# Moving one group's output stores behind the transposes of the next groups, and two matmuls one place forward, in a fused attention and MLP kernel

## Chip, cores and metric

One NeuronCore of a Trainium2 chip. The metric is the device time of one execution in microseconds (us), of the slowest core, which here is the only one.

## The reference, cut to what matters

```python
kv  = einsum('bhsd,bhse->bhde', k, v)          # 8 batches, 8 heads, 576 rows, 64 wide
out = einsum('bhsd,bhde->bhse', q, kv)
x   = out / sqrt(mean(out*out) + 1e-6) * g_norm  # -> 4608 tokens x 512
h   = x @ w_in                                  # 512 -> 2048
g   = where(h > 0, h, exp(min(h, 0)) - 1)       # ELU
y   = g @ w_out                                 # 2048 -> 512, float32 out
```

## The kernel before

The 4608 tokens are worked in nine groups T of 512. For each group: x is made (attention, scaling, and for T >= 2 four DMA transposes of x with a multiplication by the gain after them), the first product gives h, ACT and DVE make the ELU, the second product gives y, ACT copies y from PSUM, SyncE issues the stores. Batch b of Q, K, V is fetched ahead by loads from GpSimd's queue; Q is turned by DMA transposes. All DMA transposes and nearly all stores are issued from SyncE, in program order.

```python
outp = ctx.enter_context(tc.tile_pool(name="outp", bufs=3))   # y tiles, 128 x 2 x 512 f32

def scale():                       # inside attention(T), for each half h of the group
    # DVE: xs = at * ss
    for i in (2 * h, 2 * h + 1):
        nc.sync.dma_start_transpose(out=xT[T][:, :, i*P : i*P+P], in_=st["xs"][:, i, :])
def gain():                        # DVE: xT[T][half h] *= g_col
    ...
def mm2_out(T, j):
    half = j // 2
    if j % 2 == 0:
        o_sb[T, half] = outp.tile([P, 2, DM], FP32, name="o_sb", tag="o")
    nc.scalar.copy(o_sb[T, half][:, j % 2, :], o_ps[T, j])
    if j % 2 == 1:
        store(T, half)             # two DMAs of 256 KB on SyncE
# ---- group 0, first product (tiles (i, a) of h, chunk c of the 4 of the contraction) ----
    early([(2, 1)], 0)
    early([(2, 1)], 2)
    early([(0, 0), (0, 1)], 3)     # the last chunk of the first pair; then ACT may start its ELU
    early([(2, 1)], 1)
    early([(1, 0), (1, 1), (2, 0), (2, 1)], 3)
# ---- ... group 1's first product, with attention(2) in between ----
    at["mul1"]()                   # group 2's second half of x: DVE scale, two transposes
    # cut: rest of group 1's ELU
    turn_q(3)                      # two DMA transposes of batch 3's Q
    after_turn(3)                  # GpSimd waits here for them
    fetch_ahead(4)                 # loads of batch 4: Q 1152 KB, K and V 576 KB each
    # cut: second product of group 1
    at["gain0"](); at["gain1"]()
# ---- group T = 2, eight pairs i of the first product, attention(3) in between ----
    early = {2: ("sum0", "inv0"), 5: ("sum1", "inv1", "mul1"), 6: ("gain0",), 7: ("gain1",)}
    late = {0: ("kv",), 1: ("se0",), 2: ("mul0",), 4: ("se1",), 5: ("ahead",)}
    # "early" runs ahead of the pair's ELU on DVE, "late" behind it
```

## Time and profile before

| | |
|---|---|
| timed executions before the prediction | 285.20, 285.07, 284.92 us |
| the profiled execution | **286.17 us**, span of the core 284.4 us |
| PE busy | 276.9 us, 97% of the span |

The span runs from the first to the last instruction; the device time was 1.8 us above it. The page, the chain of waits, the timeline and the DMA view are quoted in the prediction below.

### The profile page before, as it was taken

What the parts mean: (1) busy time and instruction counts of PE and PEld (TensorE: products, weight loads), DVE (VectorE), ACT (ScalarE), POOL (GpSimd) and SP (SyncE); (2) the same over time, 40 slices, a digit from 0 to 9 for tenths busy, and PEclk for the clock granted to TensorE, in tenths of its full rate; (3) what the DMA queues carried; (4) which work ended last, traced back from release to release, by engine and by line L of the source; (5) the groups of instructions that cost most, each with busy time, mean ns of one, the idle gap of its engine ahead of it and who ended that gap; (6) DMA issues with size and microseconds to landing.
All of it is one profiled execution on the core that took longest, in us unless ns stands there. A gap on an engine that the chain in (4) does not pass through costs nothing.

```text
span 284.4 us, 5154 instructions
## 1 busy us (share of the span) xinstructions
PE 276.9 (97%) x2123; PEld 129.1 (45%) x2123; DVE 164.4 (58%) x222; ACT 141.4 (50%) x209; POOL 47.9 (17%) x89
## 2 busy tenths in 40 slices
PE   8899999999899999999999999999999999999994
PEld 3444444444544444444444444444444444444443
DVE  2549532966487657754785378627863786344600
ACT  3778359594468255435542555345543554333311
POOL 7743303303330033033003120000000000000000
PEclk9999999999999999999999999999999999999999
DMA  7999999999896889779627971612150234020222
GB/s 208 198 203 207 206 263 236 174 298 144 191 282 72 163 182 239 94 176 262 148 37 172 248 173 35 157 37 74 37 113 0 74 39 111 0 76 0 74 74 75
DMA packets 50571, 39.46 MB, mean 139 GB/s; under 512 B 30964, under 2 KB 44020, under 8 KB 50548
## 3 DMA queue, kind: packets, MB, share of 16 engines
q0 software_dynamic: 15008, 21.30, 37.4%
q1 hardware_dynamic: 35136, 17.31, 29.4%
q10 hardware_dynamic: 404, 0.53, 0.5%
q8 instruction: 16, 0.26, 0.3%
q14 instruction: 7, 0.06, 0.1%
HBM read 36.70 MB, written 9.44 MB: 162 GB/s over the span
## 4 chain that ended last, share of the span: by engine, by line
PE 87%; DMA 6%; DVE 2%; ACT 2%; POOL 1%; issue 0%; SPq 0%; DVEq 0%; POOLq 0%
PE h_ps L382 40%; PE o_ps L403 40%; DMA xT<-xs 3%; DMA v_bf<-in_v_dram 3%; PE at L250 2%; PE at L156 1%; PE o_ps L440 1%; PE h_ps L569 1%; ACT elu_e L350 1%; DVE gT L366 1%; POOL k_bf L90 1%; PE mean L199 0%; PE qt_ps L174 0%; PE kv_ps L156 0%; PE y_ps L189 0%; DVE ss L283 0%
## 5 line engine op out<-in xcount | busy, mean ns | idle before, releaser
L403 PE MATMUL o_ps<-w_out_sb,gT 128*128 128x512 bf16 x560 | 129.7, 379 | 0.0
L382 PE MATMUL h_ps<-xT,w_in_sb 128*128 128x512 bf16 (+1 forms) x560 | 128.0, 376 | 1.0 <-DVE xT L312 0.9
L350 ACT ACTIVATE elu_e<-h_ps 128x1024 bf16<-128x1024 f32 (+1 forms) x79 | 74.0, 952 | 90.6 <-PE h_ps L382 89.0
L403 PEld LDWEIGHTS <-gT 128*128 128x128 bf16 x560 | 54.4, 98 | 65.8 <-issue 0.9
L382 PEld LDWEIGHTS <-w_in_sb 128*128 128x128 bf16 x560 | 53.2, 98 | 62.4 <-PE o_ps L403 1.4
L366 DVE TENSOR_TENSOR gT<-elu_e,h_ps 128x1024 bf16<-128x1024 bf16 (+1 forms) x67 | 77.2, 1157 | 6.9 <-PE h_ps L382 0.5
L362 DVE TENSOR_SCALAR elu_e<-elu_e 128x1024 bf16<-128x1024 bf16 x72 | 31.2, 433 | 64.6 <-ACT elu_e L350 64.6
L419 ACT COPY o_sb<-o_ps 128x512 f32<-128x512 f32 x32 | 18.3, 587 | 21.1 <-PE o_ps L403 21.1
L103 POOL CAST q_bf<-st_q 128x384 bf16<-128x384 f32 x36 | 16.8, 508 | 41.6 <-DMA st_q<-in_q_dram 41.6
L283 DVE TENSOR_REDUCE ss<-sq 128x16 f32<-128x1024 bf16 x14 | 17.1, 1220 | 6.8 <-ACT sq L277 6.8
L299 DVE TENSOR_TENSOR xs<-at,ss 128x1024 bf16<-128x1024 f32 x14 | 17.1, 1219 | 1.9 <-ACT ss L292 1.9
L277 ACT ACTIVATE sq<-at 128x1024 bf16<-128x1024 f32 x14 | 14.4, 1029 | 0.0
L212 DVE SCALAR_TENSOR_TENSOR xT<-y_ps,g_col,rT 128x512 bf16<-128x512 f32 (+1 forms) x10 | 6.2, 641 | 10.1 <-ACT rT L209 7.9
L339 POOL COPY gate<-qT 1x16 bf16<-1x16 bf16 x5 | 1.1, 217 | 59.0 <-DMA qT<-q_bf 59.0
L355 ACT ACTIVATE elu_h<-h_ps 128x1024 bf16<-128x1024 f32 (+1 forms) x12 | 9.3, 817 | 0.0
L156 PEld LDWEIGHTS <-k_bf 64*64 64x64 bf16 x576 | 6.4, 107 | 5.5 <-issue 5.5
L312 DVE TENSOR_SCALAR xT<-xT,g_col 128x1024 bf16<-128x1024 bf16 x14 | 6.7, 480 | 3.3 <-DMA xT<-xs 3.3
L90 POOL DMA_DIRECT2D v_bf<-in_v_dram x11 | 7.7, 700 | 4.2 <-DMA w_in_sb<-in_moe_w_in_dram 2.1
L90 POOL DMA_DIRECT2D k_bf<-in_k_dram x11 | 7.7, 704 | 2.6 <-DMA w_in_sb<-in_moe_w_in_dram 1.8
L250 PEld LDWEIGHTS <-qT 64*128 64x128 bf16 (+1 forms) x248 | 4.3, 97 | 6.1 <-issue 5.9
L112 DVE COPY o_sb<-o_ps 128x256 f32<-128x256 f32 x1 | 0.4, 424 | 11.1 <-PE o_ps L440 11.1
L366 DVE TENSOR_TENSOR gT<-elu_e,elu_h 128x1024 bf16<-128x1024 bf16 x9 | 6.2, 692 | 0.8
(57 smaller groups left out, 101.3 us busy)
## 6 DMA issues: line engine op xcount, KB each, us to landing
st_q<-in_q_dram POOLq DMA_DIRECT2D x6, 1152.0 KB, 8.4
out_dram<-o_sb SPq DMA_DIRECT2D x24, 256.0 KB, 3.4
k_bf<-in_k_dram POOLq DMA_DIRECT2D x6, 576.0 KB, 10.5
v_bf<-in_v_dram POOLq DMA_DIRECT2D x6, 576.0 KB, 12.6
out_dram<-o_sb SPq DMA_DIRECT2D x19, 128.0 KB, 2.4
w_out_sb<-in_moe_w_out_dram POOLq DMA_DIRECT2D x4, 512.0 KB, 15.4
w_in_sb<-in_moe_w_in_dram POOLq DMA_DIRECT2D x2, 512.0 KB, 10.7
q_bf<-in_q_dram POOLq DMA_DIRECT2D x3, 288.0 KB, 13.4
```

The source lines that it names most:

```text
L90: eng.dma_start(out=dst.rearrange("p m j d -> p m (j d)"), in_=in_[:, ms, :])
L103: nc.gpsimd.tensor_copy(out=bf["q", b][:, u, js], in_=raw[b][:, u::2, js, :].rearrange("p l j d -> p j l d"),)
L250: nc.tensor.matmul(se_ps[lo:hi, l, (4 * i + m) * 64 : (4 * i + m) * 64 + 64], lhsT=qT[b][l * 64 : l * 64 + 64, s, u, j : j + n, :], rhs=kv ...
L277: nc.scalar.activation(sq, st["se", h], AF.Square)
L283: nc.vector.reduce_sum(out=ss, in_=st.pop(("sq", h)).rearrange("p l (m e) -> p (l m) e", e=D), axis=AX.X,)
L299: nc.vector.tensor_tensor(out=st["xs"][:, 2 * h : 2 * h + 2, :].rearrange("p i (l m e) -> p l i m e", l=2, e=D), in0=se_ps.rearrange("p l ...
L350: nc.scalar.activation(e[:, lo:hi, :], h, AF.Exp)
L362: nc.vector.tensor_scalar(out=e, in0=e, scalar1=1.0, scalar2=1.0, op0=ALU.min, op1=ALU.subtract)
L366: nc.vector.tensor_tensor(out=gT[T][:, 2 * i + lo : 2 * i + hi, :], in0=e[:, lo:hi, :], in1=h, op=ALU.add if relu else ALU.max,)
L382: nc.tensor.matmul((ps[a] if isinstance(ps, list) else ps[:, a, :])[:, cols], lhsT=w_in_sb[:, c, f * P : f * P + P], rhs=xT[T][:, c, cols] ...
L403: nc.tensor.matmul(o_ps[T, j], lhsT=gT[T][:, f, j * P : j * P + P], rhs=w_out_sb[:, f, :], start=(f == 0), stop=(f == FC - 1),)
L419: nc.scalar.copy(o_sb[T, half][:, j % 2, :], o_ps[T, j])
```

## The change

The intent: group 0's stores (1 MB) stand ahead of group 2's transposes of x in SyncE's queue and share the DMA engines with batch 3's loads. They are issued later, behind those transposes and behind Q of batch 3, and a fourth output buffer keeps the tiles meanwhile. And the first pair of group 0's first product gets its last chunk one matmul sooner, so that its ELU starts sooner.

```diff
-    outp = ctx.enter_context(tc.tile_pool(name="outp", bufs=3))
+    outp = ctx.enter_context(tc.tile_pool(name="outp", bufs=4))
@@ mm2_out
-        if j % 2 == 1:
+        if j % 2 == 1 and T > 0:
             store(T, half)
@@ first product of group 0
     early([(2, 1)], 0)
+    early([(0, 0), (0, 1)], 3)
     early([(2, 1)], 2)
-    early([(0, 0), (0, 1)], 3)
     early([(2, 1)], 1)
@@ between group 1's first and second product
     turn_q(3)
+    for half in range(2):
+        store(0, half)
     after_turn(3)
```

## The prediction

> **What bounds the kernel now.** I read the page first: the tensor engine (PE) is busy 97% of a span of 284.4 us, at full granted clock in all 40 slices. So nearly everything that can still be won is time in which PE stands still, and there is little of it.
>
> ```profile
> span 284.4 us, 5154 instructions
> PE 276.9 (97%) x2123; PEld 129.1 (45%) x2123; DVE 164.4 (58%) x222; ACT 141.4 (50%) x209; POOL 47.9 (17%) x89
> PE 87%; DMA 6%; DVE 2%; ACT 2%; POOL 1%; issue 0%; SPq 0%; DVEq 0%; POOLq 0%
> ```
>
> The 7.5 us in which PE is not busy: PE's first matmul starts at 1.2 us and its last ends at 280.5 us, so about 5 us lie before and after the stream and are not touched. Some 2.5 us are left. In the chain that ended last only one DMA wait lies behind the first 20 us, 8.6 us long, and it is for a transpose of x. In order of time, from DVE's scaling to PE's next product:
>
> ```profile
> 60.12 1.22 DVE xs L299
> ...
> 62.62 8.60 DMA xT<-xs
> ...
> 71.32 0.50 DVE xT L312
> ...
> 71.91 1.92 PE h_ps L382 x16
> ```
>
> The timeline of the same place shows what PE loses by it (the last columns are the idle time before a row and what ended it), and that two DVE gains wait for the transposes, one for each half of x:
>
> ```profile
> 71.32 0.49 DVE L312 TENSOR_SCALAR xT<-xT,g_col 128x1024 bf16<-128x1024 bf16 x1 [2.16 <-DMA xT<-xs]
> 71.91 1.92 PE L382 MATMUL h_ps<-xT,w_in_sb 128*128 128x256 bf16 x16 [0.94 <-DVE xT L312]
> 72.26 0.49 DVE L312 TENSOR_SCALAR xT<-xT,g_col 128x1024 bf16<-128x1024 bf16 x1 [0.45 <-DMA xT<-xs]
> ```
>
> PE's idle time understates the loss. A stream of 8 matmuls of 512 columns takes 1.73 us in the chain, 0.216 us each, but one is booked 0.379 us, because ends are modelled. The last product before the wait started at 70.60, so the next was due at 70.81; it started at 71.91. The loss is **1.10 us**.
>
> The same test of starts elsewhere: after the start-up (18 us) only one other start is late by more than 0.2 us, the fifth pair of the first product (group 0), waiting for the PSUM pair that the first pair's ELU frees:
>
> ```profile
> 16.88 0.88 DVE L212 SCALAR_TENSOR_TENSOR xT<-y_ps,g_col,rT 128x256 bf16<-128x256 f32 x2 [0.45 <-ACT rT L562]
> 18.62 1.03 ACT elu_e L350
> 19.68 0.44 DVE elu_e L362
> 20.21 1.23 DVE gT L366
> 21.48 7.07 PE h_ps L382 x32
> ```
>
> The matmul before 21.48 started at 21.01, so this one was due at 21.23: **0.25 us** lost. The change's two parts aim at these two places.
>
> **Why the transposes are late.** In the DMA view of 48 to 71 us, sizes and the median time from issue to landing:
>
> ```profile
> st_q<-in_q_dram POOLq DMA_DIRECT2D x1, 1152.0 KB, 11.3
> out_dram<-o_sb SPq DMA_DIRECT2D x4, 256.0 KB, 4.1
> v_bf<-in_v_dram POOLq DMA_DIRECT2D x1, 576.0 KB, 16.6
> ```
>
> Group 0's four stores (1 MB) are issued at 51.05 to 54.6; batch 3's loads of Q, K, V (2.3 MB) at 52.66, 53.41 and 54.14. V lands at 54.14 + 16.6 = 70.7. The first two transposes of x, issued at 61.37 and 62.62, took 9.1 and 8.6 us and landed at 70.4 and 71.2: when the loads were through. The next two took 4.8 and 4.0 (71.7 and 72.2). Group 3's transposes at 91.5 and 92.7, with nothing else under way, took 2.4 to 2.5. The next batch's loads, issued at 74.25, had 0.5 MB of stores beside them, not 1 MB, and landed after 7.2 (Q) and 12.5 us (V).
>
> **What the Trainium skill says.** "DMA: Bandwidth & Descriptors", section "Issuing engines are not separate DMA queues": transfers issued from several engines run on the same 16 DMA engines and interleave. Its section "Queues, rings and completion order" has each DMA engine take turns between the queues with work, a packet at a time. The trace agrees about sharing: loads lengthen from 12.5 to 16.6 us beside twice the stores. It shows that a transpose does worse than a fair turn: 8.6 to 9.1 us beside loads, 2.4 alone. "TensorE: Matmul & The Clock Gate", section "Step-by-step: what each phase is for", gives 215.7 ns between starts of 512-column matmuls; the trace has 0.216 us.
>
> **The change, part by part.** No instruction is added or removed; PE has the same 2,123 matmuls. Comparing the order of instructions, SyncE's queue now has Q's transposes for batch 2, x's four, Q's two for batch 3, then the four stores; PE swaps one matmul with two.
>
> *Stores later.* Batch 3's loads keep their issue time, since their gate waits for Q's transposes of batch 2, which are ahead of the stores in both. Without stores they should do at least as well as the next batch's: Q at 52.7 + 7.2 = 59.9, V at 54.1 + 12.5 = 66.6 (an estimate from those rows). x's first two transposes then land by 67. DVE is in order, and its last ELU piece ahead of the first gain ends at 69.16, so that gain ends at 69.7: 1.1 us before PE wants it at 70.8. The third and fourth transposes wait for DVE's second scaling (66.90) and go out at 66.9 and 68.2 as before; at the undisturbed 2.5 us the fourth lands at 70.7 and the second gain ends at 71.2. PE needs it after 8 matmuls of 256 columns, 8 x 0.108 = 0.86 us behind 70.81, at 71.7. Half a microsecond to spare. So 1.10 us go; all of it lies on PE's path, and PE has no late start over 0.15 us behind 73 us, so it should reach the end whole.
>
> *Last chunk sooner.* The pair's last matmul moves up by one, so ACT's exponential, DVE's two steps and the released pair come 0.216 us sooner. But the first of the two now starts at 17.77, just when DVE ends that chunk (16.88 + 0.88 = 17.76); DVE's signal took 0.05 us at 16.43 to 16.48, so PE loses about 0.05 there. Net 0.25 - 0.05 = **0.20 us**.
>
> *The fourth output buffer* lets the deferred tiles stay; it is no work. It also removes a wait of ACT's copy for DVE, which had long been served.
>
> Sum: 1.10 + 0.20 = 1.30 us of 285.07, so 283.8 us.
>
> **The rivals.**
>
> 1. *The crowd moves to the next group.* The stores now go out at about 73 to 75, with group 1's store and batch 4's loads: 1.5 MB of stores beside 2.3 MB. V of that batch landed at 88.2; by 1 MB at the 246 to 249 GB/s that the DMA moved over 51 to 62 and 74 to 85 us, it may come 4 us later, 92, less what its earlier gate gives. Group 3's first two transposes (issued 84.45, landed 88.8 and 89.2) could then land at 92. DVE takes the first gain at 92.41 now, in front of an ELU step that frees the PSUM pair for the group's first product at 96.23. For: the starving pattern above. Against: both marks move 1.3 us earlier, to 91.1 and 94.9, and gain (0.5) and ELU step (1.75) still fit from 92. The later two transposes are issued at 90.2 and 91.4 by then; they have 0.5 us to spare. If the loads reach 93 or 94 instead, PE stalls 0.5 to 1.0 us and the time is 284.3 to 284.8.
>
> 2. *The second gain takes the place of the first.* If x's fourth transpose takes 4.0 us as before and not 2.5, the second gain ends at 72.7 and PE stalls about 1 us between the halves: then only 0.1 to 0.3 us is won in all, 284.8. For it: Q's transposes of batch 3 run next to it as before. Against: loads should have been gone since 66.6, and group 3's transposes, also followed by Q's, took 2.5.
>
> 3. *Part two waits elsewhere:* PE arrives 0.2 us sooner at weights of the second product that land at 42.20 and are wanted at 42.67. They still fit, by 0.27 us. If not, 0.1 to 0.2 us is lost: 284.0.
>
> **Range and chances.** The repeats before spread 0.28 us. Both losses removed in full (1.35) give 283.7, so 283.4 with scatter is the floor. Rival 1 or 2 in part, about one in four together, gives up to 284.8. A change of 2% would be 5.7 us; PE's starts that were late for another engine come to 1.8 us behind the start-up (1.10, 0.25, and three of 0.09 to 0.15), and no engine receives more work. So within 2% is next to certain.
>
> **What would show it.** Right: the chain of waits has no 8.6 us transpose at 62; PE's idle 0.94 before the group 2 product is gone or below 0.1; V of batch 3 lands near 66; the first two x transposes take about 5 us, the last two about 2.5; the four stores are issued at 73 to 75; PE's 0.25 at 21 us is below 0.1; the last matmul ends 1.3 us earlier. Wrong: an idle time of PE at 95 with a release by group 3's gain or ELU (rival 1), or one at 72 between the halves (rival 2), or x's transposes still landing at 70 with the loads gone, which would mean that stores were not what held them.

## More of the kernel before

One more view of the kernel before, for later: the stretch from 56 to 59 us, in which group 0's stores and batch 3's load of Q share the DMA engines. Columns: stretch, its length, busy time of PE, of PE's weight loads, of DVE, ACT and GpSimd (with instruction counts), PE's granted clock, mean busy DMA engines' share, GB/s.

```profile
56.00:59.00 3.00, 3.00 (x30) 1.46 (x29) 1.42 (x3) 2.69 (x3) 0.00 (x0) 1.00 0.85 276
```

## The result, and the profile after

| | median | executions |
|---|---|---|
| before | 285.13 us | 284.92 to 285.43, 4 runs |
| after | 285.66 us | 285.34 to 286.30, 4 runs |

The ratio is 1.0021, 95% interval 1.0001 to 1.0040: no faster, if anything a little slower (under 2% counts as the same), and outside the predicted range. Ratios here and below are the mean time of one kernel's fast runs over the mean of the other's fast runs of the same rounds, so not quite the ratio of the medians.

The profiled execution after took 285.56 us. Its page:

```profile
span 283.8 us, 5119 instructions
PE 274.6 (97%) x2089; PEld 128.9 (45%) x2123; DVE 164.6 (58%) x222; ACT 141.5 (50%) x209; POOL 49.8 (18%) x89
PE 89%; DMA 5%; POOL 1%; issue 1%; DVE 1%; ACT 0%; SPq 0%; DVEq 0%; POOLq 0%
```

Profile against profile the change looks like a gain: the span is 0.6 us shorter. (34 matmul records are missing from this trace, so a busy PE of 274.6 us means nothing; starts on either side of a missing record look 0.216 us late, and I left such gaps out.) The timeline shows that what was predicted at 71 us happened as worked out. The two gains of group 2's x end at 69.85 and 71.54 (predicted 69.7 and 71.2), and PE's product follows with no idle time (two rows of DVE's view, then one of PE's):

```profile
69.37 0.48 DVE L312 TENSOR_SCALAR xT<-xT,g_col 128x1024 bf16<-128x1024 bf16 x1
71.05 0.49 DVE L312 TENSOR_SCALAR xT<-xT,g_col 128x1024 bf16<-128x1024 bf16 x1 [1.20 <-DMA xT<-xs]
...
70.82 1.91 PE L382 MATMUL h_ps<-xT,w_in_sb 128*128 128x256 bf16 x16
```

And rival 1 came true in front of group 3. The same view, 24 us later:

```profile
93.06 0.48 DVE L312 TENSOR_SCALAR xT<-xT,g_col 128x1024 bf16<-128x1024 bf16 x1 [1.63 <-DMA xT<-xs]
...
95.12 0.48 DVE L312 TENSOR_SCALAR xT<-xT,g_col 128x1024 bf16<-128x1024 bf16 x1
...
95.66 1.90 PE L382 MATMUL h_ps<-xT,w_in_sb 128*128 128x512 bf16 x8 [0.38 <-DVE xT L312]
```

The first gain waits 1.63 us for a transpose; the ELU step behind it and the second gain follow in DVE's order, and PE, whose last product started at 94.90, starts 0.54 us late. In the kernel before, the first gain waited for nothing here:

```profile
92.41 0.48 DVE L312 TENSOR_SCALAR xT<-xT,g_col 128x1024 bf16<-128x1024 bf16 x1
```

The reason is in the DMA view of 72.6 to 78 us, with the sizes and the median time from issue to landing: the loads of batch 4, which landed after 7.2 (Q) and 12.5 us (V) before, now share the engines with 1.5 MB of stores, which themselves take 9 us.

```profile
st_q<-in_q_dram POOLq DMA_DIRECT2D x1, 1152.0 KB, 8.7
out_dram<-o_sb SPq DMA_DIRECT2D x4, 256.0 KB, 9.0
...
v_bf<-in_v_dram POOLq DMA_DIRECT2D x1, 576.0 KB, 17.2
```

So the two profiles differ by -1.10 at 71 and +0.54 at 95, which makes the 0.6 us. But the medians differ by +0.5. Either the profile before, or that after, was not an ordinary execution.

### The profile page after: what moved, and what is told of

It reads as the page before. It is cut to its first block, busy times and chain, and to the rows that moved or that the text cites. A ratio compares the mean times of both kernels' runs of the same rounds, so it can differ in the third digit from the quotient of the medians.

```text
span 283.8 us, 5119 instructions
## 1 busy us (share of the span) xinstructions
PE 274.6 (97%) x2089; PEld 128.9 (45%) x2123; DVE 164.6 (58%) x222; ACT 141.5 (50%) x209; POOL 49.8 (18%) x89
## 4 chain that ended last, share of the span: by engine, by line
PE 89%; DMA 5%; POOL 1%; issue 1%; DVE 1%; ACT 0%; SPq 0%; DVEq 0%; POOLq 0%
PE o_ps L403 41%; PE h_ps L382 41%; DMA xT<-xs 3%; DMA v_bf<-in_v_dram 2%; PE at L250 2%; PE at L156 2%; PE h_ps L569 1%; PE o_ps L440 1%; POOL k_bf L90 1%; PE qt_ps L174 0%; PE mean L199 0%; PE kv_ps L156 0%; PE y_ps L189 0%; POOL v_bf L90 0%; DVE xT L312 0%
## 5 line engine op out<-in xcount | busy, mean ns | idle before, releaser
L403 PE MATMUL o_ps<-w_out_sb,gT 128*128 128x512 bf16 x548 | 128.4, 379 | 0.8 <-issue 0.2
L382 PE MATMUL h_ps<-xT,w_in_sb 128*128 128x512 bf16 (+1 forms) x540 | 126.4, 376 | 1.4 <-DVE xT L312 0.4
L103 POOL CAST q_bf<-st_q 128x384 bf16<-128x384 f32 x36 | 18.5, 557 | 39.2 <-DMA st_q<-in_q_dram 39.2
## 6 DMA issues: line engine op xcount, KB each, us to landing
k_bf<-in_k_dram POOLq DMA_DIRECT2D x6, 576.0 KB, 10.7
```

Of the source, the lines that this page charges most:

```text
L103: nc.gpsimd.tensor_copy(out=bf["q", b][:, u, js], in_=raw[b][:, u::2, js, :].rearrange("p l j d -> p j l d"),)
L382: nc.tensor.matmul((ps[a] if isinstance(ps, list) else ps[:, a, :])[:, cols], lhsT=w_in_sb[:, c, f * P : f * P + P], rhs=xT[T][:, c, cols] ...
L403: nc.tensor.matmul(o_ps[T, j], lhsT=gT[T][:, f, j * P : j * P + P], rhs=w_out_sb[:, f, :], start=(f == 0), stop=(f == FC - 1),)
```

## The experiments

A term used from here on: a **late start** is the time between two starts of matmuls beyond the 0.216 us (512 columns) or 0.108 us (256 columns) that a running stream shows. "Slow" means an execution of 285.45 us or more, an arbitrary line above the bulk. It is not a state of the clock: the mean granted clock is 0.997 to 1.0 in slow and quick executions alike (0.993 in one of stores_far). Each experiment gives one profile and, with five rounds, six executions. Four kernels at a time ran on one chip, with the kernel before beside them, in four sets, each on another chip: the first four below; the next four (without the stores, the same with the swap, half of the stores, the quiet stretch); the stores twice, the swap again, the changed kernel again and the last version; the swap a third time with three single looks at the changed kernel.

### The kernel before again

No edit. 

> The kernel before, unchanged, for a second profile. Theory N (the profiled execution of before was not an ordinary one): it took 286.17 us where the timed runs' median is 285.13, so an ordinary execution lacks about 1.0 us, and the place is the wait for the transposes of group 2's x. Then this profile has a span near 283.4 us and an idle time of PE before the first product of group 2 (L382, near 71 us) under 0.4 us. Theory T (the wait is always there, and the change gives back elsewhere what it wins): idle 0.9 us again, late start 1.1 us, span near 284.4 unless something else is shorter. Time: 285.1 in both; ratio 1.000.

Measured: 285.00 us median (284.89 to 285.98), ratio 0.9992 (0.9972 to 1.0011). The profile fell on an execution of 284.94 us, with a span of 283.2. At 71 us:

```profile
69.64 0.49 DVE L312 TENSOR_SCALAR xT<-xT,g_col 128x1024 bf16<-128x1024 bf16 x1 [0.55 <-DMA xT<-xs]
...
70.73 1.91 PE L382 MATMUL h_ps<-xT,w_in_sb 128*128 128x256 bf16 x16
```

PE's row has no idle time: **the wait that the change was made for was not there.** V of batch 3 landed 14.7 us after its issue, not 16.6, at 68.8 us; the first two transposes at 69.0 and 69.5. The loads in the DMA view of 52 to 60 us, and the stretch that was quoted of before:

```profile
st_q<-in_q_dram POOLq DMA_DIRECT2D x1, 1152.0 KB, 9.6
...
v_bf<-in_v_dram POOLq DMA_DIRECT2D x1, 576.0 KB, 14.7
```

```profile
56.00:59.00 3.00, 3.00 (x29) 1.47 (x29) 1.49 (x3) 2.77 (x3) 0.00 (x0) 1.00 0.94 327
```

The same program moved 327 GB/s here where the slow execution moved 276. That is theory N, as expected for it.

### The swap alone

```diff
+    early([(0, 0), (0, 1)], 3)
     early([(2, 1)], 2)
-    early([(0, 0), (0, 1)], 3)
```

> Only the swap of the last chunk's matmuls. My prediction's step: 0.20 us faster (284.9, ratio 0.9993). Theory W (the first 45 us are bound by the arrival of weights, so PE only waits at the next load): ratio 1.000 within 0.0007, and in the profile PE's late start at 21 us is below 0.1 us while a wait for w_in or w_out of 0.1 to 0.2 us has appeared before 45 us. It also is a second sample of the wait at 71 us: under 0.4 by theory N, 1.1 by theory T.

Measured: 285.90 us median (284.98 to 286.52), ratio 1.0025 (1.0005 to 1.0046); the profile fell on the fastest execution, 284.98, with no late start at 71 or 95, and the one at 21 us gone. So five of six executions were slow and the one profiled was not. Neither my step (-0.20) nor theory W (no change) covers it; what the slow ones waited for was left open until the next two.

### The stores alone

```diff
-    ... name="outp", bufs=3
+    ... name="outp", bufs=4
-        if j % 2 == 1:
+        if j % 2 == 1 and T > 0:
     turn_q(3)
+    for half in range(2):
+        store(0, half)
```

> Only the later stores with the fourth buffer. Theory N: nothing is won at 71 us in ordinary executions and about 0.5 us is lost before the first product of group 3 (near 95 us), where batch 4's loads and the stores hold up the transposes: 285.6, ratio 1.0015 to 1.003. Theory T: 1.1 won and 0.5 lost at these two places, so 284.5, ratio 0.998, and then the loss must come from the swap. If the swap is harmless and this one repeats 285.6, theory N stands.

Measured: 285.37 us median (284.93 to 286.46), ratio 1.0003 (0.9981 to 1.0025), three of six slow. Profile at 285.67 us: nothing late at 71, **0.55 us late in front of group 3**, V of batch 4 landing at 92.4. Rival 1 comes from the stores alone. The median lies lower than theory N said (285.6), presumably because some executions have no wait at 95 either; after_again below shows one such.

### The stores still later

```diff
                 def ahead(b=T + 2):       # in group 2, behind group 3's transposes
                     turn_q(b)
+                    if T == 2:
+                        for half in range(2):
+                            store(0, half)
```
with no store of group 0 elsewhere and five output buffers.

> The four stores of group 0 behind group 3's transposes and batch 4's Q (five output buffers), so that they meet neither batch 3's nor batch 4's loads. If the crowd around batch 4's loads is what costs (rival 1 of the prediction), V of batch 4 lands near 88 again and the wait before group 3 falls from 0.54 to under 0.1 us. Theory N: the time is then that of before less the little wait at 71 us, 284.8 to 285.1, ratio 0.999 to 1.000. Theory T: 284.0, ratio 0.996. If the crowd only moves to group 4, a wait shows up at 115 to 126 us instead and the ratio is above 1.001.

Measured: 286.85 us median (286.44 to 289.40), ratio 1.0070 (1.0038 to 1.0101). The wait before group 3 is gone and the crowd has moved to batch 5's loads, as the last sentence of the expectation has it: group 4's first transposes, issued at 109.4 and 111.5, landed at 119.4 and 119.8, and the gain that waits for them holds up an ELU step in DVE's order, whose PSUM pair PE needs. Timeline, and PE's clock in stretches of 1 us after it (the last column but two):

```profile
122.01 2.31 PE L382 MATMUL h_ps<-xT,w_in_sb 128*128 128x512 bf16 x8 [2.40 <-DVE gT L366]
```

```profile
123.00:124.00 1.00, 1.00 (x5) 0.36 (x3) 1.00 (x2) 0.00 (x0) 0.59 (x2) 0.67 0.86 206
124.00:125.00 1.00, 1.00 (x4) 0.34 (x3) 0.02 (x1) 0.64 (x1) 1.00 (x2) 0.50 0.96 190
...
127.00:128.00 1.00, 1.00 (x6) 0.42 (x5) 0.42 (x1) 0.00 (x0) 0.00 (x0) 1.00 1.02 332
```

In this execution (289.40) the late start was 2.56 us, and after it PE's granted clock was halved for 3.4 us, which costs half of that, 1.7 us, more: 289.40 - 2.56 - 1.7 = 285.1.

### Group 0's stores left out

```diff
-        if j % 2 == 1:
+        if j % 2 == 1 and T > 0:
```
on the kernel before. The result is wrong: 512 rows are never written.

> The kernel before with group 0's four stores left out; its first 512 output rows are wrong on purpose. It shows the most that moving them can give. Theory N2 (two profiles of before had no wait at 71 us, one had 1.1; so its executions of 285.4 to 286.4 us are those with the wait, 4 of 11, and the others have nothing to win): all executions near 284.9, spread under 0.4 us, mean 0.3 to 0.5 us under before's mean, and PE starts late neither at 71 nor at 95 us. Rival O (the slow executions of before have some other cause, in the start or in the loads): the spread of 1.4 us stays and the mean gains under 0.15.

Measured: 285.34 us median, **285.16 to 285.44**, ratio 0.9998 (0.9980 to 1.0016). The spread is 0.28 us, where before, on the same chip in the same rounds, had 284.90 to 286.55, four of eleven slow. No late start at 71 or 95. None of six against four of eleven could still be luck (about one chance in seven); with the next run and with the stores issued twice, below, it is shown that the slow executions come from the stores (theory N2). The level I had wrong: it is 0.3 to 0.4 us above the fast executions of before and the mean gains only 0.02. In the trace 4.08 us pass from PE's last end to the end of the span, where before_again's trace has 3.84; that is about half of the 0.45 us between the two profiled executions (285.39 and 284.94). I don't know why the end is longer; the kernel with the swap and without these stores has it too (4.11).

### The same with the swap

Both edits; wrong. 

> As no_stores0 (wrong on purpose), with the swap of the last chunk's matmuls. The swap alone gave 285.9, but its profiled execution took 284.98 and showed no new wait. Theory D (the swap itself is harmless; it only brings PE 0.2 us sooner to the transposes of group 2, whose slack is 0.3 to 0.5 us, so more executions wait there): without the stores the swap gives the time of no_stores0 within 0.2 us. Rival P (the swap costs by itself, by waits on weights or on the first loads): 0.4 to 0.8 us above no_stores0, with late starts of PE before 45 us.

Measured: 285.21 us median (285.18 to 285.48), ratio 0.9994 (0.9975 to 1.0014), one of six just over the line (285.48, which is the profiled one, with no late start in front of group 2 or 3). Against no_stores0 in the same rounds the mean is 0.05 us lower. Theory D: without these stores the swap does no harm. That it makes more executions wait at 71, as the expectation has it, is not shown.

### Half of the stores later

Two early as before, two behind batch 3's Q:

```diff
-        if j % 2 == 1:
+        if j % 2 == 1 and (T, half) != (0, 0):
     turn_q(3)
+    store(0, 0)
```
and four output buffers.

> Two of the four stores early as before, two behind batch 3's Q. If the harm is a matter of bytes beside each batch's loads, half a MB at each place fits both slacks: V of batch 3 lands near 67 and V of batch 4 near 90 (between 87.5 and 92.5), no late start at 71 nor at 95, every execution near 284.9. If the landing of the transposes at 95 has a threshold that half the stores pass already, 0.1 to 0.3 us is lost there: 285.1 to 285.2.

Measured: 285.01 us median (284.94 to 285.76), ratio 0.9993 (0.9973 to 1.0012), one of six slow. The profile fell on that one: V of batch 3 at 66.7 as expected and nothing late at 71, but V of batch 4 at 92.6 and PE 0.59 us late before group 3. With half the bytes the wait there is still possible; whether it is rarer (one of six slow, against three of six for stores_only in another set) is not shown. V took 15.4 us here, not 17.0 as in stores_only, but its load was issued 1.8 us later (77.22 and 75.39); more on that below.

### Two of the stores into a quiet stretch

Two early as before, two between the first and the second pair of group 3's transposes, where the DMA of before had nothing to do from 88.8 to 92.4 us (windows of its trace: 0 GB/s):

```diff
-        if j % 2 == 1:
+        if j % 2 == 1 and (T, half) != (0, 0):
-            late = {0: ("kv",), 1: ("se0",), 2: ("mul0",), 4: ("se1",), 5: ("ahead",)}
+            late = {0: ("kv",), 1: ("se0",), 2: ("mul0", "st0"), 4: ("se1",), 5: ("ahead",)}
+            at["st0"] = lambda: store(0, 0)
```
and four output buffers.

> Two stores early, two between the first and the second pair of group 3's transposes (issue near 86 us), a stretch of 88.6 to 92 us in which before's DMA had nothing to do. V of batch 4 lands at 87.5 to 88.5, no late start at 71 or 95: executions near 284.9, spread under 0.4, mean 0.3 to 0.5 under before. If the two stores hold up the second pair of transposes behind them in the same queue by over 0.5 us, PE starts late at 95 by up to 0.5 us: 285.2 to 285.4.

Measured: 285.02 us median, **284.95 to 285.24**, ratio 0.9988 (0.9971 to 1.0006), none of six slow; V of batch 3 at 67.2, V of batch 4 at 87.9, nothing late at 71 or 95. The two stores were issued at 85.84 and 86.53 and had landed by 90.2, before the second pair of transposes went out (90.28). The expected state in full, but for the level, which is 0.1 higher.

### The stores twice

The reverse: more bytes in the place that matters. Group 0's tiles are stored a second time at once, into group 7's rows, which get their right values much later.

```diff
             store(T, half)
+            if T == 0:
+                store(T, half, 7)      # same tile, rows of group 7
```

> Group 0's stores issued a second time at once, into rows of group 7 that are written over rightly much later (the result stays right): 2 MB of stores beside batch 3's loads instead of 1 MB. Without stores V of batch 3 landed at 64.8 to 65.7, with 1 MB at 68.8, 69.3 and 70.7. If stores delay loads and loads hold the transposes, V lands at 72 to 75, x's first transposes with it, and PE waits 2 to 5 us at 71 in every execution: 287 to 290, ratio 1.007 to 1.017. If the wait at 71 in the first profile of before had another cause, V and the time hardly move (ratio under 1.003).

Measured: 287.61 us median (287.20 to 288.41), ratio 1.0081 (1.0054 to 1.0109), all four slow. V of batch 3 at 71.35 (17.3 us after its issue), the first transposes at 71.6 and 71.9. PE at 71 us, in the profile of 287.20:

```profile
72.53 1.64 PE L382 MATMUL h_ps<-xT,w_in_sb 128*128 128x256 bf16 x11 [1.60 <-DVE xT L312]
```

1.76 us late here, and 0.28 more at the second half of x. Stores delay loads, loads hold the transposes, the transposes hold PE: the chain answers to its first link. It answers less than I expected (V at 72 to 75).

The middle link was not moved by itself, for no run changes the loads alone. A rival is that stores hold the transposes directly, standing ahead of them in SyncE's queue. In before_again the trace speaks against it: from 62.3 to 65 us, when both transposes had been issued (61.30 and 62.56), only the queue of the loads moved any packet:

```profile
q0 software_dynamic: 498, 0.56, 120.2%
```

Here, with the last stores landing at about 68.4, and in front of group 3 in the changed kernel, where they landed at about 88.9 and the transposes had gone out at 83.34, both may be at work.

### The swap alone, again and a third time

> The swap alone, again, for the share of slow executions (5 of 6 at 285.7 or above, against 9 of 28 of before) and another profile. Theory D (chance; the swap is harmless): about a third of the executions slow, median near 285.0, and if the profile falls on a slow one it shows V of batch 3 past 70 us and a wait at 71. Rival P (the swap makes executions slow): most of the executions above 285.5 again, and a slow profile shows the wait at some other place that the swap reaches, before 62 us.

Measured: 285.73 us median (284.85 to 287.62), ratio 1.0011 (0.9979 to 1.0043), four of six slow. This time the profile fell on the slowest, 287.62:

```profile
72.68 0.49 DVE L312 TENSOR_SCALAR xT<-xT,g_col 128x1024 bf16<-128x1024 bf16 x1 [3.06 <-DMA xT<-xs]
...
73.27 0.49 PE L382 MATMUL h_ps<-xT,w_in_sb 128*128 128x256 bf16 x3 [2.12 <-DVE xT L312]
```

```profile
st_q<-in_q_dram POOLq DMA_DIRECT2D x1, 1152.0 KB, 12.1
...
v_bf<-in_v_dram POOLq DMA_DIRECT2D x1, 576.0 KB, 17.9
```

The slow execution of the swapped kernel is the slow execution of before, with more of it: Q lands late beside the stores (65.1), V after it (72.3), the first two transposes around V (71.3 and 72.6), and PE is 2.29 us late at 71. Not one of the places that the swap reaches.

> The swap alone a third time, for the share of slow executions: 9 of 12 took 285.45 us or more, against 14 of 39 of before and none of 12 of the two kernels that have the swap and the stores out of the way (no_stores0_order and quiet_order). Chance: a third slow, so that in all 11 of 18 against 14 of 39 and this run's. Not chance: 4 to 6 of 6 slow again. Whichever profile comes: time = 285.0 (within 0.2) + late start before group 2.

Measured: 285.53 us median (284.78 to 285.97), ratio **0.9989** (0.9963 to 1.0015), three of six slow, beside seven of eleven of before in the same rounds. Profile at 285.93: V of batch 3 at 70.5, PE 1.17 us late at 71. Over all sets the swap alone had 12 slow of 18, the kernel before 21 of 54 (both over all sets). Three ratios of 1.0025, 1.0011 and 0.9989 don't settle whether that is chance; they show no loss that repeats. ("None of 12" in the expectation is one of 12: 285.48 of no_stores0_order lies over the line.)

### The changed kernel, four more times

> The changed kernel again, for a second profile. From the two profiles of deferred stores (0.54 and 0.55 us late at 95 us): median 285.4 to 285.7, ratio 1.001 to 1.002; no late start at 71, V of batch 4 landing at 92 to 93 and 0.4 to 0.7 us late at 95. If V of batch 4 lands before 91, no late start there and 285.0.

Measured: 285.89 us median (284.82 to 286.55), ratio 1.0015 (0.9990 to 1.0040). The profile fell on the fastest execution, 284.82: V of batch 4 at 91.6 instead of 92.75, and no late start before group 3. About 1 us in the landing of a load decides. ("Half of its ten executions took 286 us and more", in the next expectation, is four of ten.)

> The changed kernel, one profile. So far its profiles fell on 284.82 us (no late start of PE at 71 or 95) and 285.56 us (0.54 late at 95), while half of its ten executions took 286 us and more. Theory: the time is 285.0 within 0.2 plus PE's late starts in front of groups 2 and 3, and with stores late only group 3's is left; so an execution of 286.3 shows V of batch 4 landing past 93 us and 1.2 to 1.4 us late at 95. If a slow profile shows 0.6 or less there, the rest of its time has another place, which the profile will name.

> As after_p1: time = 285.0 (within 0.2) + late start before group 3; nothing late before group 2.

> As after_p1: time = 285.0 (within 0.2) + late start before group 3; nothing late before group 2.

These three had one profile and one execution each, so their state counts as unknown (granted clock 1.0 in all): 285.41, 286.17 and 285.32 us, 0.59, 1.41 and 0.33 us late before group 3, with V of batch 4 at 92.6, 93.3 and 92.1; none late at 71. after_p2 is the slow one:

```profile
93.64 0.48 DVE L312 TENSOR_SCALAR xT<-xT,g_col 128x1024 bf16<-128x1024 bf16 x1 [2.54 <-DMA xT<-xs]
```

```profile
96.24 1.04 PE L382 MATMUL h_ps<-xT,w_in_sb 128*128 128x512 bf16 x4 [1.25 <-DVE xT L312]
```

What made it slow was not a slower load. V of batch 4 took 16.5 us in after_p2 and 16.5 in after_again; but the loads, which wait on GpSimd until a transpose of batch 3's Q has landed, went out 1.6 us later. The gate in after_again, then in after_p2:

```profile
73.08 0.19 POOL L339 COPY gate<-qT 1x16 bf16<-1x16 bf16 x1 [11.73 <-DMA qT<-q_bf]
...
74.65 0.19 POOL L339 COPY gate<-qT 1x16 bf16<-1x16 bf16 x1 [11.34 <-DMA qT<-q_bf]
```

This happens without group 0's stores as well: the same gate opened at 75.36 in no_stores0 and at 74.60 in quiet_order below.

### Both: two stores in the quiet stretch, and the swap

> Candidate: two stores early, two in the stretch between group 3's transposes (as stores_two_quiet, whose six executions were 284.95 to 285.24), with the swap. Theory D: as stores_two_quiet, less the 0.2 us that the swap took from PE's stream in profiles: 284.8 to 285.0, no execution above 285.4. Rival P: 285.5 or more in most.

Measured: **284.95 us median, 284.84 to 285.06**, ratio 0.9984 (0.9964 to 1.0004), none of six slow, where before in the same rounds had 284.84 to 286.76 and five of eleven slow. It is correct. Timeline before group 3 and the loads of batch 4, to be held against those of the changed kernel above:

```profile
91.18 0.48 DVE L312 TENSOR_SCALAR xT<-xT,g_col 128x1024 bf16<-128x1024 bf16 x1
94.06 0.49 DVE L312 TENSOR_SCALAR xT<-xT,g_col 128x1024 bf16<-128x1024 bf16 x1 [0.74 <-DMA xT<-xs]
...
95.00 1.67 PE L382 MATMUL h_ps<-xT,w_in_sb 128*128 128x512 bf16 x7
```

```profile
st_q<-in_q_dram POOLq DMA_DIRECT2D x1, 1152.0 KB, 6.3
...
v_bf<-in_v_dram POOLq DMA_DIRECT2D x1, 576.0 KB, 11.7
```

The first gain waits for nothing, the second ends 0.45 us ahead of PE's start, PE has no idle time, and V takes 11.7 us, not 17.2. This kernel takes the place of both: its best is that of before, its worst is better by 1.7 us. By the ratio the mean gain is 0.16%, and the interval still just includes 1; what stands out is the spread: with stores_two_quiet none of 12 executions slow, where before in the same two sets had nine of 22. The profile doesn't show more room at 71 than a quick execution of before has (V of batch 3 at 69.0, first gain at 69.72; in before_again 68.8 and 69.64), so that no wait can come back there is not shown.

### One sum over the profiles

Each profiled execution has its own time, so the late starts can be held against it:

| profile | its time | late before group 2 | late before group 3 | time less these |
|---|---|---|---|---|
| before | 286.17 | 1.10 | 0 | 285.07 |
| before_again | 284.94 | 0 | 0 | 284.94 |
| after | 285.56 | 0 | 0.54 | 285.02 |
| after_again | 284.82 | 0 | 0 | 284.82 |
| after_p1 | 285.41 | 0 | 0.59 | 284.82 |
| after_p2 | 286.17 | 0 | 1.41 | 284.76 |
| after_p3 | 285.32 | 0 | 0.33 | 284.99 |
| order_only | 284.98 | 0 | 0 | 284.98 |
| order_again | 287.62 | 2.29 | 0 | 285.33 |
| order_third | 285.93 | 1.17 | 0 | 284.76 |
| stores_only | 285.67 | 0 | 0.55 | 285.12 |
| stores_half | 285.76 | 0 | 0.59 | 285.17 |
| stores_two_quiet | 284.95 | 0 | 0 | 284.95 |
| quiet_order | 284.95 | 0 | 0 | 284.95 |
| stores_twice | 287.20 | 2.04 | 0 | 285.16 |

Times from 284.8 to 287.6 shrink to 284.8 to 285.3. What separates the executions of these kernels is these two waits and little else. (Left out: the two kernels without the stores, 285.4 and 285.5 with neither wait, and the one with the stores far behind, whose wait is before another pair.)

## Why the prediction was wrong, step by step

**The base and the 1.10 us: wrong, and this is the step that failed.** "So 1.10 us go; all of it lies on PE's path." The profile showed a late start of 1.10 us, and I took it off the *median* of the timed executions, in which it is not. Of five profiles of kernels with all four stores early and once (before twice, the swap alone three times), two have no wait at 71 at all and three have 1.10, 1.17 and 2.29 us. The executions with it are a minority of before's: 21 of 54 were slow, and the median of the 54, 285.07, lies within 0.13 us of before_again's profiled execution (284.94), which has no such wait. (In the last set, on another chip, seven of eleven were slow and the median was 285.71; what is ordinary depends on the set.) The warning lay in the result: the profiled execution took 286.17, the timed ones 284.92 to 285.20. 286.17 - 1.10 = 285.07 would have told me that the median had already got rid of it. With this alone the prediction for the median would have been "nothing to win", 284.9 to 285.1, before rival 1.

**The mechanism at 71: right.** Stores hold up loads, loads hold transposes. V of batch 3 was predicted at 66.6 without the stores; it landed at 64.8 to 65.7 in all nine profiles that have the four stores later or not at all. V took 10.7 to 11.2 us where the prediction worked with 12.5; on the other hand its 16.6 us beside the stores were those of a slow execution, and before_again has 14.7. The gain was predicted to end at 69.7 and ended at 69.85. No profile of a kernel with late stores has a wait at 71.

**Rival 1: underestimated.** I gave it, with rival 2, one chance in four, and counted on 0.5 us of slack at the second pair of transposes. V of batch 4 was to land at 92; it landed at 91.6 to 93.3 in six profiles, and PE was late in five of them by 0.33 to 1.41 us. What I worked out for 93 to 94 us (0.5 to 1.0 us late) happened at 92.1 to 93.3. The place and the order of things, a gain that holds up an ELU step in DVE's queue, were as described, and so, nearly, was the landing of V; the slack behind it was not. I let the first gain (0.5) and the ELU step (1.75) fit behind a landing at 92, and gave the second pair of transposes 0.5 us to spare, but left out the second gain, which comes behind both in DVE's order: from the first gain to the product's start pass 2.6 us in all (93.06 to 95.66), so that a product due at 95.12 needs the first gain to start by 92.5. In after_again it started at 92.31, and PE was not late.

**The swap: right in mechanism, worth a little less.** Predicted -0.20. The late start of 0.25 us at 21 us is in all eight profiles without the swap and in none of the ten with it. From the wait for the second chunk of x (near 16 us) to group 1's second sum (near 36 us) PE took 20.17 us in the median without and 20.03 with it: 0.14. The rest went to weights that hadn't landed: where the stretch with the swap took 20.13 to 20.29 us (after, after_again, after_p3), PE starts 0.19 to 0.28 us late at the second product's weights near 33 us (0.10 in order_only), and in after and after_p3 another 0.16 to 0.18 us late near 17.8 us at the first product's. This is rival 3 at other places than it named: it looked at the weights that land at 42.20, while those before them, in the profile of before, landed at 32.75 for a start at 33.02. On the clock: no_stores0_order's mean is 0.05 below no_stores0's in the same rounds, and quiet_order's 0.11 below stores_two_quiet's (of another set), both within the scatter of single executions.

**Rival 2 did not happen** in the changed kernel: the fourth transpose landed in time.

**Why it came out slower.** The change trades a wait that before has in some executions for another. In profiles the wait at 71 is in three of five with early stores, the wait at 95 in five of six with all four stores late. Slow executions: 21 of 54 before, 8 of 13 after; medians 285.07 and 285.71. That the new wait is the more frequent one is not clear beyond noise: the ratios are 1.0021 (1.0001 to 1.0040) and 1.0015 (0.9990 to 1.0040), and the sets differ. What is shown is that nothing is won. What makes the loads of batch 3 slower in one execution than in another with the same program (276 or 327 GB/s in the same stretch), and the gate of batch 4 open 1.6 us later, is open; no run here varied it.

## What to carry to other kernels

Compare the profiled execution's own time with the timed ones before taking any wait off the median: if it is slower by as much as the wait, the wait belongs to that execution. A transfer that is moved out of one crowd needs a stretch where nothing else is due; look for one in the DMA columns (here between two pairs of transposes) and move only as many bytes as it holds (that all four stores would not have fitted here was not tried). And when a change removes a wait that only some executions have, look at the spread as well as the median: the version that won here has the same best execution as before and no slow ones.

## What the Trainium skill lacked or had wrong

- "DMA: Bandwidth & Descriptors", section "Queues, rings and completion order": engines take turns between queues packet by packet, from which one would expect a small transpose to get through beside large loads. It didn't: group 2's first transpose, issued at 61.1 to 61.6 us in every profile, landed when batch 3's V did, whenever that was: 65.4 with V at 64.9 (no_stores0), 69.0 with 68.8 (before_again), 70.4 with 70.7 (before), 71.3 with 72.3 (order_again). The page doesn't say how long a transpose takes beside loads; alone they took 2.4 us. The trace says where the time goes: issued at 61.30, the first one of before_again moved no packet up to 65 us (view under "The stores twice").
- "TensorE: Matmul & The Clock Gate", section "What's actually happening": the clock halves after an idle window of about 3.4 us. In stores_far it was halved for 3.4 us soon after an idle time of PE of only 2.40 us; after 2.12 us (order_again) and 1.60 us (stores_twice) it was not. One occurrence within a program; behind its end, before_again's clock was halved 2.1 us after PE's last matmul (279.33 to 281.45).
- The same page, section "Back-to-back issue gap": about 131 ns between 512-column matmuls in a sustained stream with weight loads. Here 8 such pairs take 1.73 us, 216 ns each, which is what the page calls the isolated gap.
- No page that I read warns that the profiled execution may not be the typical one; here two of the same kernel differed by 1.2 us (286.17 and 284.94), of which one wait made 1.10.
